# Five TensorE durations in a kernel's own planner, and the order in which its first tiles and weights are taken, are replaced

## The chip, the core and the metric

The kernel runs on one core of one Trainium2 chip. The metric is the device time of one launch in microseconds (us). The unchanged kernel was timed three times: 474.58, 475.62 and 477.79 us, so its median is 475.62 us. One more execution was taken by the hardware profiler, and every duration below comes from that one.

## What is computed

The reference runs an mLSTM recurrence and feeds its output to a two-layer network with an ELU between:

```python
for t in range(S):                      # B, H, S, D = 4, 8, 768, 40
    m_new  = maximum(f[t] + m, i[t])
    f_stab = exp(f[t] + m - m_new); i_stab = exp(i[t] - m_new); m = m_new
    C = f_stab * C + i_stab * outer(v[t], k[t])
    n = f_stab * n + i_stab * k[t]
    y[t] = sigmoid(o[t]) * (C @ q[t]) / maximum(abs(n @ q[t]), 1.0)
x = y as (3072 tokens, 320)
h = x @ w_in                            # w_in (320, 2048)
out = elu(h) @ w_out                    # w_out (2048, 320)
```

## The kernel before, in words

**Tiles.** The recurrence is done in chunks of 128 time steps. Tile `t0` to `t23` is one chunk of one batch, with all eight heads: number n is chunk n // 4 of batch n % 4, so t0 to t3 are the first chunk of the four batches and t4 to t7 the second. The gates of a chunk are worked out once for all batches (`gate_load`, `gate_chunk`, lines 399 to 522), just ahead of the chunk's first tile. For a tile, `attention` (line 555) does this:

- load qk and vko on SyncE's (SP's) queue (lines 527, 530)
- `products`, key by query on TensorE (PE), 16 matmuls (line 597)
- decay weights; in the first two chunks PE spreads the logarithms of the decays (`spread`, lines 628 to 638, in PSUM pool `h`) and ScalarE (ACT) takes the exponential (line 653)
- VectorE (DVE) multiplies products by decays, in two halves (line 662), and ACT, DVE or GpSimd (POOL) scales the values (line 666)
- `outputs` on PE: in a tile of chunk 0, lines 690 and 700; in later chunks line 682 (the carried state) as well
- denominators and the output gate on DVE and ACT (lines 733 to 746)
- `turn`, three transposes on PE (line 763), and the upper and lower parts of the result (line 769; then lines 773 and 776, or a subtraction on DVE)

**Conversions.** The weights are used as pairs of float32r parts, upper and lower. A conversion `c0` to `c17` loads one piece of them into the pool `wide` (3 buffers), and passes through ACT (lines 327, 332), DVE (336, 341, 346), POOL (351), ACT (357, the upper part), and for the lower part either DVE or POOL (line 361) or, for the numbers 0, 1, 5 and 6, PE (two matmuls, lines 369 and 370, in PSUM pool `h`) and ACT (line 373). The last reader of `wide` is POOL at line 351. What the numbers hold, with f the 16 slices of 128 hidden units:

- c0, c1, c2: w_in for f = 0 to 3 (c2 also holds 64 rows for f = 4 to 7); c5, c6: the rest of w_in for f = 4 to 7
- c3, c4, c7, c8: w_out for two slices each, f = 0, 1 / 2, 3 / 4, 5 / 6, 7
- c9, c10, c11: w_in for f = 8 to 11 (c11 also for 12 to 15); c12 and up: the remainder

**Feed-forward.** Nine blocks of 2 or 3 tiles (`BLOCKS`). For each slice f of a unit, `ffn` (line 784) does one step: eight matmuls of the first layer into `h` (line 816; PSUM pool `h` has two buffers, which the spreads and the conversions on PE share), ELU on ACT, ACT, DVE (lines 824, 827, 829), the upper part on ACT (832), the lower on DVE or POOL (834), and the second layer on PE, three matmuls a tile (line 843). The first unit is block 0 (t0, t1) with f = 0 to 7, the second block 1 (t2 to t4) with the same slices. The steps of the first unit are called s0 to s7 here.

**What sets the order.** Nothing is left to a compiler: the class `Plan` (line 38) is a list scheduler that runs on the host. Every piece of work is an `op` with a duration in us for each engine that may do it, the keys that it reads and writes, and a rank. `Plan.run` steps through its own clock, starts on each free engine the ready op of lowest rank (then longest tail) whose buffers are free in that clock, and so fixes the order of the instructions on every engine, SP's loads included. On the chip each engine goes through its own list in order and waits where something is late. A duration in `op` changes no instruction; it changes only the order.

The ranks come from `FIRST` (line 220) and from due times (lines 902 to 921). The names in `FIRST` get 0, 1, 2 and so on. A tile or conversion that isn't named gets a rank just above the step of the network at which its lead says that it is due, or 0.001 if it is due at the beginning. A step ranks above all that it needs. Buffers of a PSUM or SBUF pool are taken in turn.

Of the kernel before, what the change touches and what calls it, by code (L numbers as in the profile page):

```python
# [37 lines left out]
class Plan:  # L38
# [21 lines left out]
    def op(self, engines, fn, r=(), w=(), nbytes=0):  # L60
        port = "port" in engines
        engines = {e: x for e, x in engines.items() if e != "port"}
        o = Op(engines, fn, {k[:2] for k in (*r, *w)}, nbytes, port)
        o.rank = self.rank
        for k in r:
            if k in self.writer:
                o.before.add(self.writer[k])
            self.readers.setdefault(k, []).append(o)
        for k in w:
            if k in self.writer:  # L70
                o.before.add(self.writer[k])
            o.before.update(self.readers.pop(k, ()))
            self.writer[k] = o
        o.before.discard(o)
        for b in o.before:
            b.after.add(o)
        self.ops.append(o)
        return o
# [105 lines left out]
def tile_mlstm_then_elu_ffn(  # L184
# [11 lines left out]
    B, NC, R3, _, HH, L = qk.shape  # L196
# [20 lines left out]
    TMAX = max(BLOCKS)  # L217
    WMAX = max(512, W2N * DM)

    FIRST = "t0c0c4t1c1c5t2t4c3c7c11c9"  # L220

    LEAD, SPACE, LEAD_C = 4, 3, 0

# [3 lines left out]
    room = dict(  # L227
        wide=3, narrow=2, gates=2, qk=3, bb=3, vko=3, w=3, wl=2, dec=2, den=2, xf=2,
        x=3, ps_a=3, h=2, acc=3, e=2, gh=4, gl=4, os=3,
    )  # L230
    plan = Plan(room, ("qk", "bb", "e", "gh", "gl", "os"))
    op = plan.op
# [12 lines left out]
    def act(n):  # L245
        return {"ACT": 0.17 + 0.00088 * n}
# [132 lines left out]
    ident = const.tile([P, P], F32, name="ident")  # L379
# [175 lines left out]
    def attention(n):  # L555
        c, b = divmod(n, B)
# [3 lines left out]
        KQ = tuple(("qk", n, two) for two in range(2))  # L560
# [26 lines left out]
        def ps(which, *shape):  # L587
            return T("ps_a", (n, which), *shape)
# [10 lines left out]
                        start=True, stop=True,  # L599
                    )  # L600

        op({"PE": 1.25}, products, KQ + (("w", n, "room"),), tuple(("ps_a", (n, two)) for two in range(2)))

        if c < LOGS:
            op({"POOL": 0.2, "DVE": 0.08}, lambda e: eng[e].memset(va()[:, :, D:E], 1.0), (), (KV,))
# [69 lines left out]
        def outputs(e):  # L675
# [28 lines left out]
                            )  # L704

        KY = ("ps_a", (n, "y"))
        op({"PE": (1.6 if c else 0.9) + (0.36 if c < NC - 1 else 0.0)}, outputs,
           (("w", n, 0), ("w", n, 1), KV) + (KB + (("C", b),) if c else ())
           + ((KK,) if c < NC - 1 else ()), (KY, ("given", n)))
        if c < NC - 1:  # L710
# [44 lines left out]
        KX, KTP = ("x", kb), ("ps_a", (n, "tp"))  # L755
        ts = slice(slot * L, (slot + 1) * L)

        def xs(part):
            return T("x", kb, P, 3, TMAX * L, dt=F32R, part=part)[:, :, ts]
# [5 lines left out]
                    start=(t == 0), stop=(t == 2), is_transpose=True, skip_group_check=True,  # L765
                )

        op({"PE": 0.55}, turn, (("xf", n), ("ident", 0)), (KTP,))
        op(act(3 * L), lambda e: nc.scalar.copy(xs("h"), ps("tp", P, 3, L)),
           (KTP,), (KX + ("h", slot),))  # L770
        if n < PARTS_BY_PE[0]:
# [108 lines left out]
    blocks, n = [], 0  # L880
# [21 lines left out]
    rank = {}  # L902
    for i, x in enumerate(re.findall("[tc][0-9]+", FIRST)):
        rank[x] = float(i)
# [19 lines left out]
    for c in range(NC):  # L924
        plan.rank = rank[f"t{c * B}"] - 0.0005
        gate_load(c)
        gate_chunk(c)
        for b in range(B):
            n = c * B + b
            plan.rank = rank[f"t{n}"]  # L930
            load(n)
            attention(n)
# [48 lines left out]
```

## Time and profile before

| what | value |
|---|---|
| times of three runs | 474.58, 475.62, 477.79 us |
| the profiled execution, its own time | 479.09 us |
| its span, first to last instruction | 477.1 us |
| mean granted TensorE clock | 0.981 |
| PE busy, DVE busy, ACT busy, POOL busy | 96%, 73%, 64%, 19% |
| DMA, mean over the span | 111 GB/s, 52.83 MB |

How to read the profile: the time of the profiled execution is its span and some 2.0 us around it, and it lies 3.47 us above the median of the three runs. A row of the timeline gives start, length, engine, source line, operation, result and operands, shape and count, and in brackets the idle time of that engine ahead of it with what ended the wait. A row of the windows gives, for a stretch of time, its length and then the busy time of each engine, the granted TensorE clock as a share of full speed, the busy share of the DMA engines and what they moved. PEld is PE's weight load, which overlaps its matmuls. A matmul row's length is longer than its share of the pipeline: the distance from one start to the next is what a matmul costs.

### The profile page before, as it was taken

Reading aid. Unit: us, or ns where it says so; the run is one execution under the profiler, and the core shown is the slowest. Engines: PE = TensorE matmul, PEld = TensorE weight load, DVE = VectorE, ACT = ScalarE, POOL = GpSimd, SP = SyncE. Lnnn points to the kernel's source line nnn. Section 1 sums busy time; section 2 is a strip of 40 time slices with the busy share of each in tenths; the row PEclk is TensorE's granted clock in tenths of the full one; section 3 lists DMA queues with packets and bytes.
Section 4 is the critical chain, followed back from the end, with each engine's and each line's share of the span. In section 5 each row is a group of like instructions: output and inputs, shape, how many; then the busy total and the mean of one; then the engine's idle time right before and its main releaser. Section 6 shows DMA issues by size and latency. Waiting matters only on the chain.

```text
span 477.1 us, 13768 instructions
## 1 busy us (share of the span) xinstructions
PE 456.9 (96%) x5692; PEld 428.4 (90%) x5692; DVE 347.8 (73%) x729; ACT 303.1 (64%) x743; POOL 89.5 (19%) x103
## 2 busy tenths in 40 slices
PE   5977999999999989999999999999999999999996
PEld 3645889899999989999989999999999999999996
DVE  7897899997869899638995768648875475456543
ACT  5886788897876556646465546655546564645764
POOL 2421244433213131003040122102110010000000
PEclk9796999999999999999999999999999999999999
DMA  8777465534143394113642334404432030100000
GB/s 261 259 225 233 134 214 170 153 116 153 41 137 97 105 278 138 43 40 98 185 144 71 101 94 134 133 3 139 140 101 82 1 101 1 43 1 3 28 1 27
DMA packets 39389, 52.83 MB, mean 111 GB/s; under 512 B 2880, under 2 KB 31264, under 8 KB 39328
## 3 DMA queue, kind: packets, MB, share of 16 engines
q1 hardware_dynamic: 39328, 51.97, 35.2%
q8 instruction: 44, 0.72, 0.6%
q14 instruction: 17, 0.14, 0.1%
HBM read 46.56 MB, written 5.39 MB: 109 GB/s over the span
## 4 chain that ended last, share of the span: by engine, by line
PE 80%; DVE 10%; DMA 3%; issue 2%; ACT 2%; POOL 1%; SPq 1%; DVEq 0%; ACTq 0%
PE h L816 34%; PE acc L843 32%; PE ps_a L597 4%; PE ps_a L690 3%; PE ps_a L682 2%; DMA wide<-in_w_in 2%; PE ps_a L763 1%; DMA w<-f_d 1%; PE h L628 1%; PE ps_a L700 1%; PE h L632 1%; PE h L638 1%; DVE w L645 1%; DMA bb<-b_d 1%; DVE gl L834 1%
## 5 line engine op out<-in xcount | busy, mean ns | idle before, releaser
L816 PE MATMUL h<-xh,w 128*128 128x384 f32 (+1 forms) x720 | 179.1, 323 | 0.4 <-ACT e L827 0.2
L843 PE MATMUL acc<-w,gh 128*128 128x320 f32 x768 | 173.4, 312 | 0.1
L843 PEld LDWEIGHTS acc<-w,gh 128*128 128x128 f32 x768 | 127.8, 188 | 2.4 <-ACT gh L832 0.3
L816 PEld LDWEIGHTS h<-xh,w 128*128 128x128 f32 x720 | 125.6, 189 | 2.7 <-DVE e L829 1.0
L829 DVE SCALAR_TENSOR_TENSOR e<-e,h 128x384 f32<-128x384 f32 (+1 forms) x144 | 72.5, 505 | 69.8 <-ACT e L827 69.2
L843 PE MATMUL acc<-w,gl 128*128 128x320 f32 x384 | 118.7, 309 | 0.4 <-DVE gl L834 0.4
L824 ACT ACTIVATE e<-h 128x384 f32<-128x384 f32 (+1 forms) x144 | 65.4, 454 | 78.0 <-PE h L816 74.9
L816 PE MATMUL h<-xl,w 128*128 128x384 f32 (+1 forms) x432 | 112.0, 318 | 0.0
L832 ACT CAST gh<-e 128x384 fp32r<-128x384 f32 (+1 forms) x144 | 67.7, 473 | 35.1 <-DVE e L829 34.0
L834 DVE TENSOR_TENSOR gl<-e,gh 128x384 fp32r<-128x384 f32 (+1 forms) x122 | 66.3, 547 | 32.1 <-ACT gh L832 30.2
L816 PEld LDWEIGHTS h<-xl,w 128*128 128x128 f32 x432 | 76.9, 189 | 0.0
L827 ACT ACTIVATE e<-e 128x384 f32<-128x384 f32 (+1 forms) x144 | 70.5, 490 | 4.0
L843 PEld LDWEIGHTS acc<-w,gl 128*128 128x128 f32 x384 | 72.0, 188 | 0.9 <-DVE gl L834 0.8
L834 POOL TENSOR_TENSOR gl<-e,gh 128x384 fp32r<-128x384 f32 (+1 forms) x22 | 24.4, 1115 | 109.0 <-ACT gh L832 95.6
L645 DVE TENSOR_TENSOR_SCAN w<-w,ident 128x512 f32<-128x512 f32 x32 | 39.1, 1225 | 4.6 <-DMA w<-f_d 4.6
L615 ACT ACTIVATE vko<-vko 128x320 f32<-128x320 f32 x72 | 33.5, 467 | 7.7 <-DMA vko<-in_vko 7.2
L597 PE MATMUL ps_a<-qk 40*128 40x128 f32 x384 | 31.0, 304 | 6.4 <-DMA qk<-in_qk 5.1
L351 POOL TENSOR_TENSOR narrow<-narrow,wide 128x512 int32<-128x512 int32 (+1 forms) x18 | 26.5, 1474 | 55.5 <-DVE narrow L346 25.9
L597 PEld LDWEIGHTS ps_a<-qk 40*128 40x128 f32 x384 | 25.9, 204 | 11.6 <-DMA qk<-in_qk 5.1
L662 DVE TENSOR_TENSOR w<-ps_a,w 128x512 f32<-128x512 f32 x48 | 31.6, 682 | 3.1 <-PE ps_a L597 2.7
L690 PE MATMUL ps_a<-vko,w 128*32 128x41 f32 x1536 | 20.3, 207 | 0.0
L690 PEld LDWEIGHTS ps_a<-vko,w 128*32 128x32 f32 x1536 | 18.6, 114 | 1.2 <-issue 1.1
(104 smaller groups left out, 413.9 us busy)
## 6 DMA issues: line engine op xcount, KB each, us to landing
vko<-in_vko SPq DMA_DIRECT2D x24, 484.0 KB
qk<-in_qk SPq DMA_DIRECT2D x24, 448.0 KB
w<-f_d SPq DMA_DIRECT2D x32, 256.0 KB
wide<-in_w_out SPq DMA_DIRECT2D x8, 640.0 KB
wide<-in_w_in SPq DMA_DIRECT2D x8, 512.0 KB
out<-os SPq DMA_DIRECT2D x24, 160.0 KB
bb<-b_d SPq DMA_DIRECT2D x40, 80.0 KB
sum<-os SPq DMA_DIRECT2D x8, 160.0 KB
```

The source lines that it names most:

```text
L597: nc.tensor.matmul(ps(two, P, HH, L)[:, j, :], kt[rows, j, :], qt[rows, j, :], start=True, stop=True,)
L615: lambda e, fn=fn, kw=kw: nc.scalar.activation(v3()[2], v3()[2], fn, **kw), (), (KS,))
L645: nc.vector.tensor_tensor_scan(a, a, ident4.rearrange("p h t -> p (h t)"), 0.0, op0=ALU.mult, op1=ALU.add)
L662: lambda e, half=half: nc.vector.tensor_mul(w(half), ps(half, P, HH, L), w(half)),
L690: nc.tensor.matmul(y[r, h, :], w()[:, i, r], va()[:, h, :], start=not opened, stop=(i == H - 1), skip_group_check=True,)
L816: nc.tensor.matmul(h(), a[g][:, fs], m, start=(i == 0), stop=(i == len(prods) - 1))
L824: op(act(N), lambda e, h=h, ff=ff: nc.scalar.activation(ff("e"), h(), AF.Relu, scale=-1.0), (KHP,), (KE,))
L827: lambda e, ff=ff: nc.scalar.activation(ff("e"), ff("e"), AF.Exp, scale=-1.0), (), (KE,))
L829: lambda e, h=h, ff=ff: nc.vector.scalar_tensor_tensor(out=ff("e"), in0=ff("e"), scalar=-1.0, in1=h(), op0=ALU.add, op1=ALU.max),
L832: op(act(N), lambda e, ff=ff: nc.scalar.copy(ff("gh", F32R), ff("e")), (KE,), (KG,))
L834: lambda e, ff=ff: eng[e].tensor_sub(ff("gl", F32R), ff("e"), ff("gh", F32R).bitcast(F32)),
L843: nc.tensor.matmul(acc(a), x[:, sl], bw[g][:, j, :], start=(f == f0 and i == 0), stop=(f == f1 - 1 and i == 2),)
```

## The change

Two things are replaced: the durations that the planner is told for three kinds of work on PE, and the string `FIRST`.

```diff
-    FIRST = "t0c0c4t1c1c5t2t4c3c7c11c9"
+    FIRST = "t0c0c4t1c1t2t3t4c3c7c10c11"
...
-        op({"PE": 1.25}, products, KQ + (("w", n, "room"),), tuple(("ps_a", (n, two)) for two in range(2)))
+        op({"PE": 1.16}, products, KQ + (("w", n, "room"),), tuple(("ps_a", (n, two)) for two in range(2)))
...
-        op({"PE": (1.6 if c else 0.9) + (0.36 if c < NC - 1 else 0.0)}, outputs,
+        op({"PE": (1.38 if c else 0.8) + (0.32 if c < NC - 1 else 0.0)}, outputs,
...
-        op({"PE": 0.55}, turn, (("xf", n), ("ident", 0)), (KTP,))
+        op({"PE": 0.49}, turn, (("xf", n), ("ident", 0)), (KTP,))
```

By lines 902 to 921 the ranks of the early work become these; all that is not listed keeps its place:

| | before | after |
|---|---|---|
| c2 (not named, due at once) | 0.001 | 0.001 |
| t0, c0, c4, t1, c1 | 0, 1, 2, 3, 4 | 0, 1, 2, 3, 4 |
| c5 | 5 | 8.005, behind s3 |
| t2 | 6 | 5 |
| t3 | 8.002, behind s0 | 6 |
| gates of chunk 1, t4 | 6.9995, 7 | 6.9995, 7 |
| c3 | 8 | 8 |
| s0, s1, s2, s3 | 8.001 to 8.005 | 8.001 to 8.004 |
| c6 | 8.006 | 8.006 |
| c7, s4 | 9, 9.001 | 9, 9.001 |
| taken early, at the lowest rank | c11 10, c9 11 | c10 10, c11 11 |
| due with f = 8, rank just above 9 | c10, c12 | c9, c12 |

## The prediction

> **What bounds the kernel now.** I read the busy shares first, then the windows by stage, then the chain of waits, then the timelines of the first 62 us.
>
> ```profile
> PE 456.9 (96%) x5692; PEld 428.4 (90%) x5692; DVE 347.8 (73%) x729; ACT 303.1 (64%) x743; POOL 89.5 (19%) x103
> ```
>
> PE is the bound: 477.1 - 456.9 = 20.2 us of the span are all that it is idle. The windows say where:
>
> ```profile
> 0.00:12.00 12.00, 6.62 (x36) 4.21 (x37) 8.52 (x30) 6.35 (x14) 2.58 (x12) 1.00 0.83 261
> 12.00:24.00 12.00, 10.85 (x249) 7.86 (x249) 9.90 (x22) 10.21 (x25) 5.38 (x6) 0.79 0.77 257
> 24.00:36.00 12.00, 8.55 (x159) 5.50 (x150) 11.02 (x30) 10.12 (x24) 3.43 (x4) 0.93 0.76 224
> 36.00:48.00 12.00, 8.47 (x132) 6.12 (x130) 9.25 (x26) 7.83 (x18) 2.29 (x2) 0.64 0.76 235
> 48.00:60.00 12.00, 12.00 (x90) 10.73 (x90) 9.79 (x19) 9.53 (x23) 3.38 (x3) 0.93 0.50 138
> 60.00:96.00 36.00, 35.24 (x718) 31.79 (x718) 33.92 (x75) 30.16 (x73) 15.44 (x17) 1.00 0.57 181
> 96.00:450.00 354.00, 351.94 (x4162) 339.59 (x4161) 254.49 (x508) 214.12 (x532) 57.03 (x62) 1.00 0.30 92
> 450.00:477.10 27.10, 23.25 (x174) 22.56 (x172) 10.88 (x26) 14.80 (x38) 0.00 (x0) 0.98 0.04 13
> ```
>
> Second column: PE's busy time. The first four rows hold 48 - 34.49 = 13.51 us of idle PE, and the low clock. The long middle (96 to 450) has 2.06 us idle in 354, the tail 3.85 us. So whatever a new order can win lies before 48 us, and there the largest single hole is this one:
>
> ```profile
> 40.73 0.59 PE L628 MATMUL h<-mask,ident_b 128*128 128x512 bf16 x1 [3.53 <-DVE e L829]
> 40.27 0.41 DVE L829 SCALAR_TENSOR_TENSOR e<-e,h 128x256 f32<-128x256 f32 x1
> ```
>
> PE waits 3.53 us for the ELU step of s0 on DVE, because t4's first spread takes over the `h` buffer that s0 holds. DVE isn't idle: it is busy for 11.02 of the 12 us before 36, and the chain of waits stays on it up to this step. And after the hole PE is slow:
>
> ```profile
> 40.70:44.00 3.30, 3.27 (x18) 1.97 (x19) 2.24 (x6) 2.09 (x5) 1.45 (x1) 0.50 0.63 178
> 44.00:47.20 3.20, 3.20 (x111) 2.88 (x109) 1.88 (x4) 1.97 (x4) 0.72 (x1) 0.50 0.94 282
> 47.20:49.50 2.30, 2.30 (x15) 2.30 (x12) 1.87 (x6) 0.84 (x4) 0.17 (x1) 0.50 0.85 202
> ```
>
> 8.8 us go by at half the granted clock, so some 4.4 us are lost beside the 3.53.
>
> **The durations.** They add and remove no instruction. In the plan's own clock PE gets shorter by 24 x 0.09 (products) + 4 x 0.14 + 16 x 0.26 + 4 x 0.22 (outputs of chunk 0, of chunks 1 to 4, of the last) + 24 x 0.06 (turns), 9.2 us. On the chip nothing of that is time; it only shifts what the plan puts beside what. What these cost on the chip:
>
> ```profile
> 51.31 1.09 PE ps_a L597 x16
> 13.21 0.74 PE ps_a L690 x64
> 13.95 0.29 PE ps_a L700 x32
> ```
>
> Products 1.09 us against 1.25 planned before and 1.16 after; outputs of t0, at full clock, 0.74 + 0.29 = 1.03 us against 1.26 and 1.12. The new figures are nearer, so the order in the middle can hardly get worse by them. Bounds there: a gain of at most the 2.06 us idle, a loss of one new hole like the 3.53 one. I take 0, since the plan made with the worse figures left only 2.06.
>
> **t3 goes from rank 8.002 to 6, ahead of t4's gates and of s0.** Its steps on PE and DVE in the profile (first the outputs, at half clock, then the DVE work):
>
> ```profile
> 45.46 1.25 PE ps_a L690 x64
> 46.71 0.55 PE ps_a L700 x32
> 40.60 1.28 DVE L662 TENSOR_TENSOR w<-ps_a,w 128x512 f32<-128x512 f32 x2
> 47.54 0.17 DVE L737 TENSOR_SCALAR den<-den 128x8 f32<-128x8 f32 x1
> 47.74 0.20 DVE L738 RECIPROCAL den<-den 128x8 f32<-128x8 f32 x1
> 48.15 0.48 DVE L742 TENSOR_TENSOR vko<-vko,den 128x320 f32<-128x320 f32 x1
> 48.77 0.49 DVE L746 TENSOR_TENSOR xf<-ps_a,vko 128x320 f32<-128x320 f32 x1
> ```
>
> Term A: t3's outputs leave the slow stretch, 1.25 + 0.55 = 1.80 us there, and go, at the 1.03 us of full clock, into PE's idle time before 37 us (24 to 36 us: 3.45 us idle). Bounds 0 and 1.80; I take 1.80, since the idle time there is three times what is put in. They can come that early only if t3's products do, and these hang on a load:
>
> ```profile
> 24.01 0.33 SPq L322 DMA_DIRECT2D wide<-in_w_out  x1
> 24.39 1.30 SPq L527 DMA_DIRECT2D qk<-in_qk  x2
> 32.26 1.16 PE L597 MATMUL ps_a<-qk 40*128 40x128 f32 x16
> ```
>
> c3's load (24.01) waits in SP's queue for POOL to give a `wide` buffer back, and t3's qk, the first of the two at 24.39, is behind it. With rank 6 it is to stand ahead of it, so the products at 32.26 can be several us earlier. What moves back on SP's queue is then c3's load, by one issue (half of the 1.30), against a wait for a buffer that it has anyway.
>
> Term B: 1.28 + 0.17 + 0.20 + 0.48 + 0.49 = 2.62 us of DVE work now stand ahead of the L829 that PE waits for, in a stretch in which DVE has no idle time. A cost of 2.62, less what c5 takes away:
>
> **c5 goes from rank 5 to 8.005, c3 so takes its turn.** c5's rows on DVE:
>
> ```profile
> 31.46 0.39 DVE L336 TENSOR_SCALAR narrow<-narrow 128x512 f32<-128x512 f32 x1
> 31.88 0.43 DVE L341 TENSOR_SCALAR narrow<-narrow 128x512 int32<-128x512 int32 x1
> 32.34 0.69 DVE L346 SCALAR_TENSOR_TENSOR narrow<-wide,narrow 128x512 int32<-128x512 int32 x1
> ```
>
> 1.51 us leave the stretch before s0's L829, while c3 stays ahead of it. B is 2.62 - 1.51 = 1.11 us of loss; bounds 0 (DVE finds room elsewhere) and 2.62 (c5 is converted early all the same). I take 1.11.
>
> Term C: c5's lower part is made by PE in an `h` buffer,
>
> ```profile
> 35.78 1.02 PE L369 MATMUL h<-narrow,ident 128*128 128x512 f32 x2
> 38.17 0.57 ACT L373 CAST w<-h 128x512 fp32r<-128x512 f32 x1
> 47.26 3.17 PE h L816 x16
> ```
>
> and holds the second one from 35.78 to 38.74, right behind s0, which holds the first. With c5 gone from there, s1's first layer can have that buffer while PE has nothing else. Today s1 and s2 are the 16 matmuls at 47.26, 3.17 us. Filling the hole with s1 takes two thirds of that from the slow stretch (eight at half clock, then eight partly at full), 2.1 us. Bounds 0 (the plan puts the spreads first again) and 2.1; I take 2.1, because s0's and c5's buffers are what the wait at 40.73 shows.
>
> Term D, the clock after the hole. The new hole is 3.53 + 1.11 (B) - 1.03 (t3's outputs) - 0.95 (s1 at full clock, as below) = 2.66 us. Bounds: nothing gained (the clock still halves), or what A and C leave of the slow stretch, 8.8 - 1.80 - 2.1 = 4.9 us, runs at full clock, a gain of half of it, 2.4 us. I take 0 by this row:
>
> ```profile
> 16.00:19.00 3.00, 1.85 (x12) 0.95 (x10) 2.87 (x6) 2.95 (x7) 0.00 (x0) 0.98 0.99 356
> 19.00:22.00 3.00, 3.00 (x21) 2.15 (x22) 2.93 (x6) 2.97 (x9) 1.29 (x1) 0.50 0.49 147
> 52.88 0.95 PE h L816 x8
> ```
>
> Here 1.15 us of idle PE within 3 us, in pieces, sufficed for half clock.
>
> The Trainium skill, TensorE: Matmul & The Clock Gate, "What's actually happening", says that the clock halves after an idle window of about 3.4 us, a window that runs freely. By it a hole of 2.66 us leaves the clock up and the sum is larger by D's 2.4 us; the trace agrees at 40.7 us (3.53 idle) and disagrees at 19 us.
>
> c9 and c10 change places behind c11 and c10; all three are conversions of one kind at the lowest rank, needed from f = 8 on, and PE is full there: 0.
>
> **Sum.** 1.80 - 1.11 + 2.1 + 0 = 2.8 us less: 479.09 becomes 476.3 for an execution like the profiled one. That one lies 3.47 us above the median, so the median goes from 475.62 to **472.8 us**. DVE caps it: between 40.7 and 49.5 it is idle for 8.80 - 5.99 = 2.81 us, and s4 can't come before c5 and c6 are through it.
>
> **The rivals.**
>
> *Warm clock.* The hole closes or stays too short for the clock to halve; D's 2.4 us come on top, 470.4 us. For it: s1 and t3 fill most of the hole. Against: the row at 19 us, and DVE's cap.
>
> *DVE takes it back.* The start is bound by DVE and ACT, whatever PE does. A and C save nothing, since s4 waits for the same conversions, and B's 1.11 us stays or is hidden: 475.6 to 476.7. For it: DVE has 11.02 of 12 us busy from 24 to 36, and 33.92 of 36 from 60 to 96. Against: its 2.81 us idle above.
>
> *c6 late (slower).* Its lower part is ready just in time for s4:
>
> ```profile
> 51.67 0.68 DVE L346 SCALAR_TENSOR_TENSOR narrow<-wide,narrow 128x512 int32<-128x512 int32 x1
> 56.51 0.82 DVE L346 SCALAR_TENSOR_TENSOR narrow<-wide,narrow 128x640 int32<-128x640 int32 x1
> 56.97 0.56 ACT L373 CAST w<-h 128x512 fp32r<-128x512 f32 x1
> 58.31 0.28 PE L816 MATMUL h<-xh,w 128*128 128x256 f32 x1
> ```
>
> c5 now comes just ahead of c6. If it takes c6's turn on DVE and c6 the next, 56.51 - 51.67 = 4.84 us later, s4 is as late. t4's outputs, at the least the 1.03 us of t0's, fill a part; 3.8 us are idle, and half clock after that costs up to 4.4 us as now: 8.2 us lost, less up to 2.8 won before, 481.0 to 483.8. It decides from c6 being more than 58.31 - 57.53 + 1.03 = 1.8 us later. Against: c5 and c3 only swap `wide` buffers, and c6's buffer, c1's, comes free as before.
>
> **How the numbers follow.** Forecast 0.45, warm clock 0.2, DVE takes it back 0.2, c6 late 0.15. The forecast's own range, from the bounds of A, B and C, is a gain of 3.9 to a loss of 2.6 at the very ends, 471.7 to 478.2. The range for all reaches down past the warm clock with A, B and C at their best (475.62 - 3.9 - 2.4 = 469.3, and a little of the middle's idle) and up to just under the slow case: 468.5 to 480.5. A change of 1% (4.8 us) is about what a measurement of this kernel can tell from none: below 470.9 falls most of the warm clock and the forecast's lowest edge, 0.24; above 480.4 most of c6 late, 0.14; within, 0.62.
>
> **What would show it.** Right: L690 of t3 (the fourth without L682) starts before 37 us; t3's qk is issued before c3's `wide`; two first layers of 256 columns run before t4's spreads; the 3.53 us wait for L829 is shorter; PE's busy time from 0 to 48 us is above 34.5 with more matmuls. Wrong: a DVE wait as long at the same place; PE idle between 54 and 68 us ahead of s4's first layer; or any change of the 351.94 us busy in the middle by more than 2 us, which would mean that the durations did more than the order.

## The result and the profile after

The changed kernel takes 480.13 us (median of 17 runs, 477.26 to 485.21) against 477.32 us (17 runs) for the kernel before. The ratio is 1.0055 [1.0031, 1.0078]: slower by some 2.6 us, where 2.8 us of gain were forecast. This ratio and all that follow leave out runs that took over 1.5% longer than the fastest of the same kernel. The profiled execution took 480.06 us, with a span of 478.1. Here is the share of the engines, from the page of the kernel after:

```profile
PE 456.9 (96%) x5692; PEld 428.0 (90%) x5692; DVE 354.6 (74%) x740; ACT 301.9 (63%) x738; POOL 85.3 (18%) x97
```

PE has the same 5692 matmuls and 456.9 us as before. The same four stages follow in windows (length, then busy us of PE, PEld, DVE, ACT and POOL with counts, granted clock, DMA share, GB/s). Before:

```profile
0.00:50.00 50.00, 36.49 (x567) 25.69 (x568) 39.83 (x106) 35.17 (x82) 13.91 (x23) 0.83 0.78 242
50.00:72.00 22.00, 21.73 (x404) 19.16 (x402) 20.34 (x43) 19.16 (x50) 8.49 (x8) 1.00 0.55 174
72.00:140.00 68.00, 67.47 (x698) 64.65 (x697) 59.11 (x123) 56.90 (x131) 21.65 (x20) 1.00 0.38 122
140.00:450.00 310.00, 307.98 (x3858) 296.31 (x3857) 217.62 (x432) 177.10 (x447) 45.48 (x53) 1.00 0.30 91
```

After:

```profile
0.00:50.00 50.00, 36.57 (x588) 27.13 (x590) 40.64 (x107) 34.87 (x82) 12.70 (x23) 0.86 0.80 234
50.00:72.00 22.00, 20.48 (x383) 16.66 (x379) 19.21 (x46) 17.84 (x47) 8.36 (x8) 1.00 0.56 171
72.00:140.00 68.00, 66.32 (x681) 63.05 (x682) 62.92 (x120) 58.01 (x130) 18.89 (x15) 1.00 0.38 124
140.00:450.00 310.00, 308.95 (x3865) 297.22 (x3865) 220.62 (x444) 175.81 (x443) 45.38 (x51) 1.00 0.30 92
```

The first 50 us hold 21 matmuls more at a higher clock. Between 50 and 140 us PE is busy for 86.80 us instead of 89.20, so 2.4 us are lost there; from 140 to 450 us it is busy for 0.97 us more. To compare unlike matmuls, I counted each one issued up to a time at its start-to-start distance at full clock ("matmul work" below, an estimate that is good to some 0.3 us). At 50 us after leads before by 1.4 us of it, at 140 us it trails by 2.45. In a second profile of after (e16) the two are +3.3 and -1.0. So a gain of the forecast kind was there at 50 us, and some 4 us were lost between 50 and 140 in both.

PE's timeline after, at the places that the prediction named:

```profile
30.23 0.30 PE L690 MATMUL ps_a<-vko,w 128*32 128x41 f32 x10 [2.59 <-issue]
35.47 0.81 PE L690 MATMUL ps_a<-vko,w 128*32 128x41 f32 x64
39.64 0.38 PE L816 MATMUL h<-xh,w 128*128 128x256 f32 x1
43.97 0.38 PE L628 MATMUL h<-mask,ident_b 128*128 128x512 bf16 x1 [3.12 <-DVE e L829]
62.04 0.39 PE L816 MATMUL h<-xh,w 128*128 128x256 f32 x1 [0.35 <-ACT w L373]
72.07 0.44 PE L816 MATMUL h<-xh,w 128*128 128x384 f32 x1 [1.12 <-DVE e L829]
```

t3's outputs start at 35.47, s1's first layer runs at 39.64 ahead of t4's spread, and the hole at the spread is 3.12 us where it was 3.53. But s4's first layer starts at 62.04 (58.31 before), and at 72.07 the next block waits for DVE. The 2.59 us in t2's outputs, with no wait for data, are new. SP's queue took t3's qk ahead of c3's load, as forecast:

```profile
15.32 0.43 SPq L527 DMA_DIRECT2D qk<-in_qk  x1
20.70 0.35 SPq L322 DMA_DIRECT2D wide<-in_w_out  x1
```

PE's waits after 50 us (total, times, longest), first after, then before:

```profile
PE h L816 <- DVE e L829: 2.8, 6, 1.1
PE acc L843 <- DVE gl L834: 0.5, 1, 0.5
PE h L816 <- ACT w L373: 0.4, 1, 0.4
```

```profile
PE ps_a L597 <- issue: 1.3, 1, 1.3
PE ps_a L763 <- DVE xf L746: 0.4, 1, 0.4
PE acc L843 <- DVE gl L834: 0.4, 1, 0.4
PE h L628 <- DVE e L829: 0.3, 1, 0.3
```

Six waits for the ELU step on DVE, 2.8 us together, stand where this profile of before has 0.3 us. A second profile of before (e12) has such waits too, three ahead of L816, 1.2 us together.

### The profile page after: what moved, and what is told of

Same layout as the page of the kernel before. It is cut to its first block, busy times and chain, and to the rows that moved or that the text cites. A ratio compares the mean times of both kernels' runs of the same rounds, so it can differ in the third digit from the quotient of the medians.

```text
span 478.1 us, 13786 instructions
## 1 busy us (share of the span) xinstructions
PE 456.9 (96%) x5692; PEld 428.0 (90%) x5692; DVE 354.6 (74%) x740; ACT 301.9 (63%) x738; POOL 85.3 (18%) x97
## 4 chain that ended last, share of the span: by engine, by line
PE 78%; DVE 13%; ACT 3%; issue 2%; DMA 2%; SPq 1%; DVEq 0%
PE h L816 32%; PE acc L843 30%; PE ps_a L597 4%; PE ps_a L690 3%; PE ps_a L682 2%; DVE w L645 2%; DVE e L829 2%; DVE gl L834 2%; PE ps_a L763 1%; DMA vko<-in_vko 1%; PE h L369 1%; PE ps_a L700 1%; DVE vko L742 1%; PE h L638 1%; PE h L632 1%
## 5 line engine op out<-in xcount | busy, mean ns | idle before, releaser
L816 PE MATMUL h<-xh,w 128*128 128x384 f32 (+1 forms) x720 | 178.5, 323 | 3.2 <-DVE e L829 2.8
L816 PEld LDWEIGHTS h<-xh,w 128*128 128x128 f32 x720 | 125.4, 189 | 6.4 <-DVE e L829 4.5
L829 DVE SCALAR_TENSOR_TENSOR e<-e,h 128x384 f32<-128x384 f32 (+1 forms) x144 | 72.5, 506 | 65.3 <-ACT e L827 64.4
L816 PE MATMUL h<-xl,w 128*128 128x384 f32 (+1 forms) x432 | 112.3, 319 | 0.3 <-ACT xl L776 0.3
L816 PEld LDWEIGHTS h<-xl,w 128*128 128x128 f32 x432 | 77.1, 190 | 0.5 <-ACT xl L776 0.5
L645 DVE TENSOR_TENSOR_SCAN w<-w,ident 128x512 f32<-128x512 f32 x32 | 41.2, 1289 | 2.9 <-DMA w<-f_d 2.6
L597 PE MATMUL ps_a<-qk 40*128 40x128 f32 x384 | 29.7, 297 | 5.1 <-DMA qk<-in_qk 5.1
L597 PEld LDWEIGHTS ps_a<-qk 40*128 40x128 f32 x384 | 24.9, 199 | 9.5 <-DMA qk<-in_qk 5.1
```

What stands on the lines that cost most here:

```text
L597: nc.tensor.matmul(ps(two, P, HH, L)[:, j, :], kt[rows, j, :], qt[rows, j, :], start=True, stop=True,)
L645: nc.vector.tensor_tensor_scan(a, a, ident4.rearrange("p h t -> p (h t)"), 0.0, op0=ALU.mult, op1=ALU.add)
L816: nc.tensor.matmul(h(), a[g][:, fs], m, start=(i == 0), stop=(i == len(prods) - 1))
L829: lambda e, h=h, ff=ff: nc.vector.scalar_tensor_tensor(out=ff("e"), in0=ff("e"), scalar=-1.0, in1=h(), op0=ALU.add, op1=ALU.max),
```

## The experiments

The last column adds up PE's gaps of over 0.15 us between 50 us and the tail that end with another engine's work. It doesn't follow the ratios closely: e11 and e18 have more such waits than before and aren't slower.

| kernel | start of `FIRST` | its end | durations | ratio to before | s4 at, us | waits, us |
|---|---|---|---|---|---|---|
| before (second profile: e12) | old | c11c9 | old | 1 | 58.3 (58.6) | 1.3 (1.5) |
| e17 | new | c11c9 | old | 1.0045 [1.0017, 1.0072] | 60.1 | 4.4 |
| e11 | old | c10c11 | old | 0.9973 [0.9933, 1.0012] | 55.9 | 3.0 |
| e18 (e11 again) | old | c10c11 | old | 0.9929 [0.9896, 0.9962] | 54.7 | 2.5 |
| e1 | new | c10c11 | old | 1.0000 [0.9967, 1.0033] | 60.4 | 1.3 |
| e2 | old | c11c9 | new | 1.0084 [1.0044, 1.0123] | 57.8 | 3.5 |
| after (second profile: e16) | new | c10c11 | new | 1.0055 [1.0031, 1.0078] | 62.0 (60.1) | 3.6 (3.7) |

**The whole change taken apart: e1, e2, e17, e18.** e1 is after with the durations of before, e2 before with the durations of after.

> The new FIRST with the old durations. If the loss comes from the order of the first tiles and conversions (s4 starting 3.7 us later, because c5 takes c6's turn), this is as slow as the whole change, ratio 1.004 to 1.008, with s4's first layer at 61 to 63 us. If it comes from the new durations, this is 0.997 to 1.002, since the head start of 1.4 us stays.

> The new durations with the old FIRST. If the durations are to blame (PE's waits for L829 in the middle, 100 to 140 us), ratio 1.003 to 1.008 with some 1 us of such waits after 96 us. If the order of the start is to blame, 0.998 to 1.002 and s4's first layer at 58 to 59 us as before.

The order alone does nothing, 1.0000; the durations alone cost 0.84%. The theory that the order is to blame for the loss fell. But the order is two things:

```diff
-    FIRST = "t0c0c4t1c1c5t2t4c3c7c11c9"
+    FIRST = "t0c0c4t1c1t2t3t4c3c7c11c9"     (e17)
+    FIRST = "t0c0c4t1c1c5t2t4c3c7c10c11"    (e11, e18)
```

> Old durations; FIRST with t3 ahead and c5 put off as in the change, but ending in c11c9 as before. Theory (the order's start wins 1.4 to 3.3 us, s4 comes late, and without the new durations no waits for DVE follow after 72 us): ratio 0.995 to 1.001, s4's first layer starting between 59 and 63 us, waits of PE after 50 us together below 2 us. Rival (the order's start brings the later waits by itself, and in the kernel with the whole new order the tail made up for them): 1.004 or more, waits after 50 us together 3 us or more.

> The kernel of e11 once more (before, with FIRST ending in c10c11). If e11's 0.9973 was a real gain: 0.995 to 0.999 again, interval below 1. If it was a draw: 0.999 to 1.003.

Its start alone costs 0.45% and brings late waits of 4.4 us without any new duration, so the rival of e17 holds. What sets e17 apart from e1 arises later: both have the same order of matmuls on PE up to 98 us, and only behind that does e17 fall back, by 1.4 us of matmul work at 140 us. Its end alone, c10 ahead of c11 and c9 left out, gains 0.27% (e11, whose interval holds 1) and 0.71% (e18). The mean of the two logarithms, -0.49%, and +0.45% give -0.04%, which is e1's 1.0000. The new durations on top of the new order cost 0.55% (after against e1). Of these parts, the prediction had the start as the gain and the other two at nothing. The end of `FIRST` alone is the version that beats both kernels in e18: 474.99 us (7 runs) against 478.15 for before beside it.

**The two moves undone one at a time: e3, e4.** e3 is after with c5 back at its old place, e4 after with t3 back at its due time.

```diff
-    FIRST = "t0c0c4t1c1t2t3t4c3c7c10c11"
+    FIRST = "t0c0c4t1c1c5t2t3t4c3c7c10c11"   (e3)
+    FIRST = "t0c0c4t1c1t2t4c3c7c10c11"       (e4)
```

> The whole change, but c5 back at its old place ahead of t2; t3 stays ahead of t4. If c5 put off is the cause, s4's first layer is back at 58 to 59 us or earlier and the ratio to before falls to 0.994 to 1.000. If t3 put first is the cause (2.6 us of DVE work ahead of s0), the ratio is 1.005 or more.

> The whole change, but t3 back at its due place behind s0; c5 stays put off. If c5 put off is the cause, s4's first layer is at 61 us or later and the ratio is 1.004 to 1.010, the head start being gone as well. If t3 put first is the cause, the ratio is 0.997 to 1.002.

1.0186 [1.0138, 1.0233] and 1.0119 [1.0067, 1.0172]. Neither is better than after (e4's interval overlaps after's slightly), so with the new durations neither move is the fault by itself. In e3 s4 starts at 57.0 us, earlier than before, and yet e3 is slower than after; in e4 it starts at 62.4. So the start of s4 doesn't decide the time.

**Which duration: e5, e6, e7.** All have the new `FIRST`. e5 takes the new durations for outputs alone, e6 those for products and turns alone, e7 moves all five the other way (1.34, 1.0, 1.82, 0.40 and 0.61).

> New FIRST; of the durations only that of the outputs is new (6.6 us of the plan's clock), products and turns keep the old ones. If shorter planned PE durations take the slack away that DVE and ACT need, PE's waits for DVE and ACT after 50 us lie between the 1.3 us of the kernels with the old figures and the 3.5 to 4.6 us of those with the new ones, nearer the latter, and the ratio to before is 1.002 to 1.008. If it is only chance which PE bursts meet a late fetch of instructions, the waits for DVE and ACT tell nothing and the time goes with the stalls at the three-quarter mark of each 256 PE instructions.

> New FIRST; of the durations only products and turns are new (3.6 us of the plan's clock). Slack theory: waits for DVE and ACT after 50 us 1.3 to 3 us, ratio 0.999 to 1.004. Chance theory: as likely above 1.005 as below 0.995.

> New FIRST; the durations are moved as far the other way (products 1.34, outputs 1.82 or 1.0 with 0.40, turns 0.61). Slack theory: PE's waits for DVE and ACT after 50 us stay at 1.3 us or less, ratio 0.994 to 1.001. Chance theory: anything from 0.99 to 1.015, with waits of up to 4 us.

1.0026 [0.999, 1.0063], 1.0161 [1.0115, 1.0207] and 1.0112 [1.0062, 1.0163]. e6 with part of the new figures is slower than after with all, and figures that are too long are no remedy. That speaks against the theory that shorter figures take slack out of the plan. Each set of figures gives another order on PE from the 164th to the 295th of its 5692 matmuls on (17 to 27 us, against e1), and that order falls well or badly.

**Does any new plan cost? e9, e10, e11.** Before, with one small edit each: products 1.24 instead of 1.25 (e9), turns 0.54 instead of 0.55 (e10), the end of `FIRST` (e11).

> The kernel before with one figure moved by a hundredth: products 1.24 in place of 1.25. It says nothing new of the hardware, but the plan comes out with another order in many places. If any new plan costs, whatever it is made for, because the chip leaves the plan's clock at places that no plan knows (late fetches, half clock, late DVE), the ratio is 1.003 to 1.015, like that of the whole change. If the changed figures or the new FIRST are themselves to blame, the ratio is 0.998 to 1.002.

> The kernel before with turns 0.54 in place of 0.55, the same test with another figure. Any new plan costs: 1.003 to 1.015. The figures or FIRST to blame: 0.998 to 1.002.

> The kernel before with only the end of FIRST changed (c10 and c11 in place of c11 and c9). The start up to 60 us stays. Both theories of the start give 0.998 to 1.002; if any new plan costs, 1.001 to 1.01, in proportion to the smaller part of the order that moves (a third of that of the other two).

1.0007 [0.997, 1.0044], 1.0017 [0.9983, 1.005] and 0.9973 [0.9933, 1.0012]. So a new order late in the plan doesn't cost by itself. Of the start these three say nothing: their PE issues before's order up to 81 us (e9, e10) and 103 us (e11). That the start of before is a lucky or well-tuned one is a rival that stays open: of the kernels with another order at the start or with other durations, none that does all the work came out below 1.0000.

**The stall without a wait: e8, e13, e12, e16.** The 2.59 us in after stand at 0.75 of a block of 256 PE instructions, counted from the start, as do all such gaps inside a group of matmuls. (Five gaps of 0.6 to 1.3 us ahead of the first matmul of an outputs group, as at 25.41 us in e13, don't; what ends those the profile doesn't show.) e13 adds 40 idle matmuls, 160 PE instructions, ahead of the first products of after; e8 added 64 to e3.

```diff
+            if n == 0:
+                for i in range(40):
+                    nc.tensor.matmul(
+                        ps(0, P, HH, L)[0:32, 0, 0:E], ident[:, 0:32], ident[:, 0:E],
+                        start=True, stop=True, skip_group_check=True,
+                    )
```

> The order of e3 (c5 early, new durations) with 64 idle matmuls, 128 PE instructions with their weight loads, put ahead of the first products, where PE waits 5 us for its first load: they move every later PE instruction by half a block of 256 and nothing else; the output doesn't depend on them. If PE's stalls inside its bursts of small matmuls are late fetches of instructions, the five stalls of e3 (28.2, 62.3, 180.1, 187.6 and 246.7 us, 5.4 us) go or turn up at other places, again at the three-quarter mark, and the ratio falls from 1.019 to 1.007 to 1.014. If they belong to the work at these places (a wait that the profile doesn't show), they stay at the same instructions and the ratio stays at 1.014 to 1.023.

> The whole change with 40 idle float32 matmuls ahead of the first products, where PE waits for its first load. One of them is two matmuls and two weight loads, so 160 PE instructions: every later one moves by five eighths of a block of 256. The 64 of e8 were 256 instructions, a whole block, so that run was no test but the control of this one: all its stalls stayed at the same instructions. If the stalls are late fetches of instructions, those of the change at 30.2 us (2.59 us) and 79.0 us are gone, any new one stands again at the three-quarter mark of the new count, and the ratio falls from 1.0055 to 0.997 to 1.003. If they belong to the instructions there, the 2.59 us stall stays in t2's outputs and the ratio at 1.003 to 1.008.

> The kernel before, profiled once more. If a late fetch of PE's instructions belongs to the order, the stall of 1.27 us at 177 us (16.75 blocks of 256 instructions) is there again within 0.5 us of its length, and no other of more than 0.5 us; if it is chance from run to run, it is gone or elsewhere.

> The whole change, profiled once more. If the late fetch belongs to the order, the stall in t2's outputs at 30 us is there again, 1.5 to 3.5 us; if it is chance from run to run, it is gone. Waits for DVE and ACT after 50 us: 3 to 4.5 us again.

e8 (1.0169 [1.0119, 1.0219]) tells nothing but that it is level with e3: each of these matmuls counts as four instructions, so the shift was one whole block, and four of the five stalls of e3 stayed at the same matmuls; the fifth, 0.41 us, is absent. In e13 the stall left t2's outputs and came back in t3's products (L603 there is L597, six lines down):

```profile
28.96 0.94 PE L603 MATMUL ps_a<-qk 40*128 40x128 f32 x12 [2.02 <-issue]
```

So the place is set by the count of instructions. Its ratio, 1.0042 [1.0005, 1.0079], lies inside after's interval, though it had a stall as well. And in e16, after once more, the stall at 30 us is absent while 477.0 us of span remain, 1.1 us less than with it. Before's own stall varies as well, 1.27 us at 177 us in its first profile and 0.99 in e12, where 0.90 more stand at 242. The stall is real, but two profiles of one kernel differ by less than it lasts, so it isn't shown to be the 2.6 us.

**Less work for DVE: e14, e15.** After and before, each without most of the lower part of the hidden layer (`gh` stands in for `gl` in the second layer from the block's second tile on), which takes some 31 us off DVE (354.6 to 323.5 us in after, 347.8 to 317.3 in before).

```diff
-                    ff("gl", F32R), ff("e"), ff("gh", F32R).bitcast(F32)),
+                    ff("gl", F32R)[:, 0:L], ff("e")[:, 0:L], ff("gh", F32R)[:, 0:L].bitcast(F32)),
...
-                    for i, (x, bw) in enumerate(((gh, w2l), (gh, w2h), (gl, w2h))):
+                    for i, (x, bw) in enumerate(((gh, w2l), (gh, w2h), (gh if a else gl, w2h))):
```

> The whole change with less work for DVE in the same order: the lower part of the hidden units is worked out for the first tile of a block alone, 128 of 256 or 384 columns, and the second layer reads the upper part in its place for the other tiles. DVE has some 35 us less to do, PE as many matmuls as before. If PE's waits for DVE eat the change's head start, they fall below 1.5 us after 50 us, and the ratio of this run to the next one is 0.990 to 1.000. If late fetches and the clock make the difference, this one stays 1.003 to 1.008 above the next.

> The kernel before with the same work left out as in the run above. DVE theory: 0.992 to 1.000 of the kernel before, its own waits for DVE after 50 us being only 1.3 us. The other theory: the same; the two are told apart by the run above.

0.9961 [0.9932, 0.999] and 0.9951 [0.9919, 0.9982], so the one over the other is 1.0010, or 1.0007 by their medians, where it was 1.0055. With a freer DVE most of the difference is gone. PE's waits after 50 us fell to 1.8 us in e14, where less than 1.5 was expected, and to 0.4 in e15. That speaks for DVE as what after runs into, but the two intervals overlap widely, and an effect of 0.3% would not be seen.

**What the clock does to one and the same order.** e9, e10, e11 and e18 issue exactly before's instructions on PE up to 81 us at the least, and on DVE and ACT up to 74 us. Yet their s4 starts at 54.5, 54.6, 55.9 and 54.7 us, and before's at 58.3 and 58.6. Before, in windows of 3.41 us or twice that:

```profile
29.14:32.55 3.41, 2.01 (x8) 0.96 (x10) 3.28 (x9) 3.22 (x9) 1.29 (x1) 1.00 1.02 280
32.55:35.97 3.42, 2.58 (x28) 2.16 (x27) 3.26 (x9) 3.01 (x7) 2.10 (x2) 1.00 0.54 161
35.97:39.38 3.41, 1.23 (x4) 0.47 (x3) 3.14 (x11) 2.56 (x7) 0.00 (x0) 1.00 0.58 202
39.38:42.79 3.41, 2.06 (x8) 0.99 (x8) 3.02 (x6) 2.14 (x5) 1.56 (x1) 0.50 0.77 259
42.79:49.62 6.83, 6.83 (x128) 6.28 (x127) 4.25 (x12) 3.46 (x9) 0.96 (x2) 0.50 0.85 228
```

e18:

```profile
29.15:32.56 3.41, 1.58 (x4) 0.67 (x4) 3.31 (x8) 3.22 (x9) 1.29 (x1) 1.00 1.02 279
32.56:39.38 6.82, 6.82 (x32) 5.14 (x31) 6.38 (x19) 4.90 (x13) 2.16 (x2) 0.50 0.62 204
39.38:42.79 3.41, 1.95 (x17) 1.14 (x17) 3.35 (x7) 3.20 (x8) 1.58 (x1) 1.00 0.78 265
42.79:49.62 6.83, 6.83 (x158) 6.32 (x156) 6.36 (x18) 6.44 (x16) 1.57 (x3) 1.00 0.81 220
```

The windows of the two lie at the same times. PE was busy for 2.01 us of the first one before and for 1.58 us in e18, and only in e18 the clock halved next. In e18 PE then did its work ahead of the hole at half speed, which cost nothing, since DVE set the end of the hole; the hole itself shrank:

```profile
40.70 0.41 DVE L829 SCALAR_TENSOR_TENSOR e<-e,h 128x256 f32<-128x256 f32 x1
41.16 0.38 PE L628 MATMUL h<-mask,ident_b 128*128 128x512 bf16 x1 [1.47 <-DVE e L829]
44.70 0.39 PE L816 MATMUL h<-xh,w 128*128 128x256 f32 x1
54.73 0.28 PE L816 MATMUL h<-xh,w 128*128 128x256 f32 x1
```

DVE's L829 starts at 40.70, later than before's 40.27, and the hole is 1.47 us instead of 3.53. After it the clock stays up, and s1 starts at 44.70 against 47.19, 2.5 us earlier. So this opening has two courses. Both profiles of before show the late one, at 479.09 and 479.88 us; the four others show the early one, at 475.25 to 477.60 us. That timed runs of before fall into the early one too is argued from these six profiles, since no profile of before itself shows it. The mean clock of an execution can't tell the course: e9 and e11 have the early one at a clock of 0.980, before the late one at 0.981. Of 105 timed runs of before (median 477.6), the 31 at 0.981 or 0.982 took 479.1 us on average, the 29 at 0.984 to 0.986 476.1 and the 36 above that 476.8.

## Why the prediction was wrong

**The failed steps: the order's gain was priced in one execution's slow stretch, and the durations were put at 0.** Taken apart, the order alone, for which the sum A - B + C gave a gain of 2.8 us, is level in the timed runs (e1, 1.0000 [0.9967, 1.0033]); the durations on top of it cost 0.55%, 2.6 us, where 0 was taken. A further 1.7 us of the 7.3 between 472.8 and 480.13 us is the base: the median of before is 475.62 us over three runs and 477.32 over 17.

A (1.80) and C (2.1) counted t3's outputs and s1 as leaving a stretch at half clock, and D the clock's 8.8 us. The prediction says that the profiled execution lies 3.47 us above the median (1.77 by the 17 runs), and uses that only to shift the sum. It was a sign that the stretch itself may belong to a slow course. e1 bears that out: its profiled execution has a span of 473.8 us, 3.3 us less than before's profiled one and near the forecast, yet it lies near its own kernel's median (475.63 against 476.02 us), and the timed runs of the two kernels are level. Measured against the early course (e9, e11, e18), after's matmul work at 50 us is 0.9 to 2.2 us behind, and e16's between 0.3 behind and 1.0 ahead. In executions of the early course there was little or no such gain to be had. How many of before's timed runs took it isn't known.

**A and C, what they do.** Both steps came as described: t3 at 35.47, s1 at 39.64 in the hole. Against the late course they gave +1.4 and +3.3 us at 50 us, with 2.8 forecast.

**B.** Forecast: the spread is 1.11 us later. In e16 it starts at 41.98 against 40.73, 1.25 later, near that size; that it comes from the rows named there isn't shown. In after it is 3.24 us later, and there the 2.59 us stall lies ahead of it.

**D.** Taken as nothing gained, from a hole of 2.66 us. The hole was 3.12 us (3.70 in e16), and half clock followed for one window of 3.41 us instead of three:

```profile
42.08:45.49 3.41, 1.52 (x13) 1.03 (x13) 2.92 (x8) 1.79 (x5) 0.12 (x1) 1.00 0.36 81
45.49:48.91 3.42, 3.42 (x19) 3.42 (x17) 3.20 (x7) 2.33 (x6) 0.72 (x1) 0.50 0.91 291
```

In this profile one more window at half clock, 31.84 to 35.26 us, follows the 2.59 us stall; e16 has none there. The rival *warm clock* so came true in part: after's timed runs have a mean granted clock of 0.990 against 0.985 for before. That is some 2.3 us more at full clock (0.0049 x 478), and yet after is slower.

The prediction set the row at 19 us against the Trainium skill, TensorE: Matmul & The Clock Gate, "What's actually happening", which has the clock follow an activity window of 3413 ns that runs freely. The traces are with the page on the window: before 70 us every stretch at half clock is one to four times 3.41 us long. They aren't with its idle window: 1.15 us of idle PE in one window sufficed at 19 us, 1.89 (3.41 - 1.52) at 45.49 after. At 40.7 us too the prediction misread the row as agreeing: by the windows above the clock fell at 39.38, inside the hole, behind a window with PE busy for 1.23 us.

**The rival that happened: c6 late.** Its mechanism, with another size: c5 now passes DVE (L346) as the conversion next ahead of c6, c6 is late, ACT makes its lower part (L373) late, and s4 waits for that. DVE's and ACT's timelines after:

```profile
46.72 0.68 DVE L346 SCALAR_TENSOR_TENSOR narrow<-wide,narrow 128x512 int32<-128x512 int32 x1
53.79 0.68 DVE L346 SCALAR_TENSOR_TENSOR narrow<-wide,narrow 128x512 int32<-128x512 int32 x1
```

```profile
55.22 0.59 ACT L373 CAST w<-h 128x512 fp32r<-128x512 f32 x1 [1.07 <-PE h L370]
61.39 0.59 ACT L373 CAST w<-h 128x512 fp32r<-128x512 f32 x1
```

The first of each pair is c5, the second c6. c6 is 2.12 us later on DVE than before (51.67), over the 1.8 us from which the rival was said to decide. Most of the rest arises on PE, whose matmuls for c6's lower part now stand behind two spreads of decays. Here they are after, then before, 3.72 us apart:

```profile
59.33 1.10 PE L369 MATMUL h<-narrow,ident 128*128 128x512 f32 x2
55.61 1.02 PE L369 MATMUL h<-narrow,ident 128*128 128x512 f32 x2
```

s4 is 3.7 us later than in the late course (1.8 in e16), and 4.2 to 7.5 us later than in the early one. The price was too high, 8.2 us gross: other work filled most of the wait on PE, which is 0.35 us, and the clock stayed at 1.00 from 50 to 72 us. Where the argument went wrong is "Against: c5 and c3 only swap `wide` buffers": the turn on DVE and ACT moves as well, whatever buffer is free. A late s4 alone is not the loss, though: e1 has it at 60.4 us and is level.

**The durations and the end of `FIRST`, both put at 0.** The bounds for the durations, a gain of 2.06 and a loss of 3.53 us, held for the change as a whole (after against e1, +0.55%, 2.6 us). Alone they exceeded it slightly: +0.84%, 4.0 us. The point value failed: "the order in the middle can hardly get worse by them" took nearness to the chip's figures for a better plan. In e1 the new order gets over its late s4; from 72 to 140 us it keeps PE busy all the time, where after has 66.32 of 68:

```profile
72.00:140.00 68.00, 68.00 (x707) 65.75 (x706) 58.84 (x125) 57.24 (x133) 21.06 (x20) 1.00 0.46 139
```

DVE is busy for 58.84 us there in e1 and for 62.92 in after: with the new order the new figures put more of DVE's work into this stretch, and PE waits for DVE's ELU step. With the old order they don't (e2, 57.73 us), and PE has only 66.15 us there all the same, so DVE's load isn't shown to be the cause. "Any change of the 351.94 us" was the wrong test: it is 351.68 in after, while the durations cost 2.6 us. The change of c9 and c10 was worth -0.27% and -0.71%, not 0. In the profiles e11 and e18 win only 0.6 and 0.9 us against before after 60 us, less than their ratios. Whether they also fall into the early course more often than before, with the same order on PE up to 103 us, 19 timed runs don't tell.

**What stays open.** Why the end of `FIRST` gains, by which steps; which of the late waits belong to which of the five figures; how often before takes which course; whether its start is just a well-tuned one; and, between the first profiles alone, why after is 1.0 us of span longer when the medians differ by 2.8 us. That last is as it should be if many timed runs of before take the early course, but no profile of before shows it.

## What to carry to other kernels

When the profiled execution is slower than the median, find out which stretch makes it so before any gain is priced in that stretch; a price at half clock holds only for the executions that have it. A planner's figure that is nearer to the chip doesn't make a better order: each edit draws a new order, worth from -0.7 to +1.9% here, so take the parts apart and time them, and see first how far a part leaves the old order as it is. Where a step is put off, follow its turn on each engine, not only its buffer.

## What the runs showed of the hardware

- From 7 to 70 us, clock changes lie on a grid of 3.41 us whose phase differs between runs (before and e18 have the same one and still part ways). In the 20 traces, in that stretch, every full-clock window with PE busy for less than 1.6 us was followed by half clock, and none with more than 2.6; in between both happened.
- Gaps on PE without any wait (0.3 to 2.6 us), inside groups of matmuls, stand at 0.75 to 0.76 of a block of 256 PE instructions (matmuls, weight loads and the few semaphore instructions of PE), and end 1.2 to 1.7 us after a 16 KB packet of the "instruction" queue. That PE waits for its instructions there is argued from the two, not shown. They don't come in every run: 2.59 us at 30 us in after, none there in e16.
- One float32 matmul of the idle ones in e8 and e13 counts as four PE instructions, two matmuls and two weight loads:

```profile
1.36 5.34 PE L597 MATMUL ps_a<-ident 128*32 128x41 f32 x80 [1.36 <-POOL ident masks.py:199]
```

The 40 calls stand as x80 on PE, with a weight load to each.
